# Sigmoid attention and a swish layer on one core: a hand-ordered kernel written anew as a table of tasks

## The chip, the cores and the metric

The kernel runs on one core of a Trainium2 chip. The metric is the device time of one execution in microseconds (us). A core has TensorE (PE, the matmuls), ScalarE (ACT, here the sigmoids), VectorE (DVE), GpSimd (POOL, which here issues the loads) and SyncE (SP, which here issues the stores). TensorE writes to PSUM, which has eight banks; ScalarE and VectorE read it.

## The reference

Eight sequences of 448 tokens, 12 heads of 64 columns; then two dense layers over all 3584 tokens, 768 to 2048 to 768. There is no softmax: each weight of the attention is a sigmoid by itself.

```python
scores = scale * np.matmul(q, k.transpose(0, 1, 3, 2)) - np.log(S)
attn = 1.0 / (1.0 + np.exp(-scores))
x = np.matmul(attn, v)                         # to (B * S, H * D)
h = x @ w_in
g = h * (1.0 / (1.0 + np.exp(-beta * h)))
out = g @ w_out
```

## The kernel before

All inputs are cast to 16 bits by the loads. The eight sequences are called batches (b); the 12 heads of a batch make three groups of four heads (`g`, 24 in all), and a group has two slots of two heads. The work comes in these units:

- **Loads and transposes.** `load_one` and `load_v` (L111, L132, L139) bring q, k and v; `load_w_in` and `load_w_out` (L149, L157) the weights. VectorE transposes q and k of a group in blocks of 32 (L177, L193).
- **Scores.** The 448 keys are three blocks of 128 and a last one of 64 (`jt` = 0 to 3). `visit` computes one block of a group in 8 matmuls of 448 columns (L208; four of them lie side by side in the array); the last block of two groups goes together, in 16. ScalarE then takes the sigmoid of two heads at once, 128 x 896 (L219). For batch 0, `half_visit` does the same with the queries in two halves of 224 columns.
- **Attention output.** `attend` sums over the keys in 16 matmuls (L278), and VectorE casts the result to `xT` (L287).
- **First layer.** `dense1(b, dc)`: 128 of the 2048 hidden columns of one batch, 6 matmuls of 448 columns (L296), a sigmoid on ScalarE (L304), a product on VectorE (L307) into `gt`. For batch 0 it is done in halves of 224 columns.
- **Second layer.** 28 tiles of 128 tokens. Tiles 0, 1, 2 and 27 are plain (`dense2`, L326): 16 matmuls of 384 columns for each half of the output, tile 27 split into 512 and 256. The other 24 go by pairs through `strassen` (L408): seven products of 8 matmuls of 384 columns in place of eight, with sums of hidden blocks (L397) and of weight blocks (L372) and sums of results (L427 and following) on VectorE.

The order is written by hand. The main loop goes over the visits; between them it takes units of the two layers from one stream (`filler_stream`), by a budget of microseconds for each visit. In the start-up, as long as no weights are there, matmuls on zeros (`idle_units`, L521, 28 in all) stand between the half visits. PSUM is split by use: three double banks for scores and two single ones in the start-up, then two double ones and four single ones (`share_psum`); `bank` hands out the single ones in turn, and `held` keeps those that a pair of tiles adds up in.

```python
for g in range(QPB):
    for second in range(2):
        half_visit(g, 0, second)
        if 2 * g + second < 2 * QPB - 1:
            idle_units(4 if g < QPB - 1 else 2)
```

Of the kernel before, what the change touches and what calls it, by code (L numbers as in the profile page):

```python
# [9 lines left out]
FP16 = mybir.dt.float16  # L10


@with_exitstack
def kernel(
# [10 lines left out]
    nc = tc.nc  # L25
    AF = mybir.ActivationFunctionType
    ALU = mybir.AluOpType

    B, H, S, D = q.shape
    NTOK, DM = out.shape  # L30
    DFF = moe_w_in.shape[1]
    P = 128
    BLK = 32
    HQ = P // BLK
    NB = S // BLK
    PAIR = D // BLK
    JF = S // P
    KL = S - JF * P
    NF = JF * P // BLK
    NPAIR = H // 2  # L40
    QPB = H // HQ
    NHC = DM // P
    NDC = DFF // P
    HALF = DM // 2
    WIN = 2 * S
    NTILE = WIN // P
    QH = S // 2
    MSCALE = 1.0 / math.sqrt(D)
    NEG_LOG_S = -math.log(float(S))
    NSLOT = B * NPAIR  # L50
    NQUAD = B * QPB

    const = ctx.enter_context(tc.tile_pool(name="const", bufs=1))
    rawp = ctx.enter_context(tc.tile_pool(name="rawp", bufs=3))
    vp = ctx.enter_context(tc.tile_pool(name="vp", bufs=2))
    qTp = ctx.enter_context(tc.tile_pool(name="qTp", bufs=4))
    kTp = ctx.enter_context(tc.tile_pool(name="kTp", bufs=4))
    attnp = ctx.enter_context(tc.tile_pool(name="attnp", bufs=12))
    xTp = ctx.enter_context(tc.tile_pool(name="xTp", bufs=3))
    sump = ctx.enter_context(tc.tile_pool(name="sump", bufs=3))  # L60
    sigp = ctx.enter_context(tc.tile_pool(name="sigp", bufs=3))
    outp = ctx.enter_context(tc.tile_pool(name="outp", bufs=4))
    psum = {}
    used = {}
    held = {}

    def share_psum(pools: ExitStack, n_sc: int, n_one: int):
        for name, bufs in (("sc", n_sc), ("one", 1)):
            psum[name] = pools.enter_context(
                tc.tile_pool(  # L70
                    name=f"ps_{name}{n_sc}",
                    bufs=bufs,
                    space=bass.MemoryType.PSUM,
                    reuse_waits="tile",
                )
            )
        used.clear()
        used.update((i, i - n_one) for i in range(n_one))

    def touch(i: int):  # L80
        used[i] = max(used.values()) + 1


    def bank(name: str, cols: int = S, hold=None):
        i = min((i for i in used if i not in held.values()), key=used.get)
        touch(i)
        if hold is not None:
            held[hold] = i
        return psum["one"].tile([P, cols], FP32, tag=f"one{i}", name=name)


    nlogs = const.tile([P, 1], FP32, name="nlogs")
    dummy = const.tile([P, 1], FP32, name="dummy")
    beta_in = const.tile([BLK, P], FP32, name="beta_in")
    beta_sb = const.tile([P, BLK], FP32, name="beta_sb")
    w_in16 = const.tile([P, NHC, DFF], FP16, name="w_in16")
    w_out16 = const.tile([P, NDC, DM], FP16, name="w_out16")

    raws = {}
    vs = {}

    def load_one(g: int, r: int, c0: int = 0, c1: int = NB, h0: int = 0, h1: int = HQ):
        b, t = divmod(g, QPB)
        if g not in raws:
            raws[g] = rawp.tile([P, 2, NB, D], FP16, tag="raw", name="raw")  # L110
        nc.gpsimd.dma_start(  # L111
            out=raws[g][h0 * BLK : h1 * BLK, r, c0:c1].rearrange("p c d -> p (c d)"),
            in_=(q, k)[r][b, HQ * t + h0 : HQ * t + h1].rearrange(
                "h (p c) d -> (h p) (c d)", c=NB
            )[:, c0 * D : c1 * D],
        )

    def load_qk(g: int):
        load_one(g, 0)
        load_one(g, 1)  # L120

    def swapped(g: int) -> int:
        return int(g > QPB and g % 2 == 1)

    def last_base(s: int) -> int:
        return (s % 2 ^ swapped(s // 2)) * KL

    def load_v(b: int):
        vs[b] = vp.tile([P, H, JF + 1, D], FP16, tag="v16", name="v16")
        rows = v[b].rearrange("h (p c) d -> p h (c d)", c=NB)  # L130
        for i in range(HQ):
            nc.gpsimd.dma_start(  # L132
                out=vs[b][i * BLK : (i + 1) * BLK, :, 0:JF].rearrange("p h j d -> p h (j d)"),
                in_=rows[:, :, JF * i * D : JF * (i + 1) * D],
            )
        rows = v[b].rearrange("h (p c) d -> p h c d", c=NB)
        for c in range(NF, NB):
            lo = (c - NF) * BLK
            nc.gpsimd.dma_start(out=vs[b][lo : lo + BLK, :, JF], in_=rows[:, :, c])  # L139

    def double_v_last(b: int):
        nc.vector.tensor_copy(out=vs[b][KL:P, :, JF], in_=vs[b][0:KL, :, JF])

    WCH = 8
    WOUT = 2

    def load_w_in(c: int):
        n = DFF // WCH
        nc.gpsimd.dma_start(  # L149
            out=w_in16[:, :, c * n : (c + 1) * n],  # L150
            in_=moe_w_in[:, c * n : (c + 1) * n].rearrange("(c p) f -> p c f", p=P),
        )

    def load_w_out(c: int, half: int):
        n = NDC // WOUT
        cols = slice(half * HALF, (half + 1) * HALF)
        nc.gpsimd.dma_start(  # L157
            out=w_out16[:, c * n : (c + 1) * n, cols],
            in_=moe_w_out[c * n * P : (c + 1) * n * P, cols].rearrange("(c p) f -> p c f", p=P),
        )  # L160

    qT = {}
    kT = {}
    at_tiles = {}
    xTs = {}

    def in_order(b: int, t):  # L170
        t = t.rearrange("p c e -> p (c e)").bitcast(FP32)
        return t.rearrange("p (q c) -> p c q", c=NB) if b == B - 1 else t

    def transpose_q(g: int, c0: int = 0, c1: int = NB, rows=slice(0, P)):
        if g not in qT:
            qT[g] = qTp.tile([P, NB * BLK, PAIR], FP16, tag="qT", name="qT")
        nc.vector.transpose(  # L177
            out=in_order(g // QPB, qT[g][rows, c0 * BLK : c1 * BLK]),
            in_=raws[g][rows, 0, c0:c1].rearrange("p c d -> p (c d)").bitcast(FP32),
        )  # L180

    def transpose_k(g: int, last: int, rows=slice(0, P)):
        if g not in kT:
            kT[g] = kTp.tile([P, S, PAIR], FP16, tag="kT", name="kT")
        to = kT[g][rows].rearrange("p k e -> p (k e)").bitcast(FP32)
        frm = raws[g][rows, 1].rearrange("p c d -> p (c d)").bitcast(FP32)
        frm = frm.rearrange("p (c f) -> p c f", c=NB)
        if last:
            to, frm = to[:, JF * P :], frm[:, NF:].rearrange("p c f -> p (c f)")
        else:  # L190
            to = to[:, 0 : JF * P].rearrange("p (j i q) -> p i j q", j=JF, i=HQ)
            frm = frm[:, 0:NF].rearrange("p (i j) f -> p i j f", j=JF)
        nc.vector.transpose(out=to, in_=frm)  # L193

    def transpose(g: int, r: int):
        if r == 0:
            transpose_q(g)
        else:
            transpose_k(g, 0)
            transpose_k(g, 1)  # L200

    def score_tile():
        return psum["sc"].tile([P, 2, 512], FP32, tag="sco", name="sco")

    def score(sco, u0: int, s: int, jt: int, hh: int, e: int, c0: int, n: int):
        g, lo = s // 2, (s % 2 * 2 + hh) * BLK
        base, nk = (last_base(s), KL) if jt == JF else (0, P)
        nc.tensor.matmul(  # L208
            sco[base : base + nk, hh, u0 : u0 + n],
            kT[g][lo : lo + BLK, jt * P : jt * P + nk, e],  # L210
            qT[g][lo : lo + BLK, c0 : c0 + n, e],
            start=(e == 0),
            stop=(e == PAIR - 1),
            tile_position=(lo, base),
        )

    def weigh(sco, n: int):
        at = attnp.tile([P, 2, S], FP16, tag="attnT", name="attnT")
        nc.scalar.activation(  # L219
            out=at[:, :, 0:n],  # L220
            in_=sco[:, :, 0:n],
            func=AF.Sigmoid,
            bias=nlogs[:, 0:1],
            scale=MSCALE,
        )
        return at


    def visit(g: int, jt: int, also=()):
        if jt < JF:  # L230
            todo = [(score_tile(), [s]) for s in (2 * g, 2 * g + 1)]
        else:
            todo = [(score_tile(), [2 * h, 2 * h + 1]) for h in (g, *also)]
        for e in range(PAIR):
            for sco, slots in todo:
# [82 lines left out]
    def dense2(t: int, half: int, part: int):  # L318
# [14 lines left out]
        if part < N2 - 1:  # L333
            return
# [343 lines left out]
```

## Time and profile before

| | |
|---|---|
| time, median of 3 runs | 391.84 us (390.23 to 391.84) |
| the profiled execution: time, span | 392.5 us, 390.7 us |
| mean granted TensorE clock | 0.996 |
| busy: TensorE, ScalarE, VectorE, GpSimd | 98%, 62%, 59%, 17% |
| chain that ended last: TensorE, ScalarE, VectorE, DMA | 94%, 2%, 1%, 1% |
| matmuls; sigmoids of scores; second-layer products | 2988; 171; 672 and 128 plain |
| loaded into the core, HBM read | 22.81 MB, 45.62 MB |

The span is the time from the first to the last instruction of the profiled execution; the time holds 1.8 us more. The groups of the profile are by source line, engine and shape, with the busy time of all and the mean of one; an instruction of ScalarE or VectorE overlaps the next one by some 0.1 us, so a mean is longer than the distance from start to start. In the timeline a line holds several instructions of one kind in a row.

### The profile page before, as it was taken

How to read it: one execution, taken by the hardware profiler on the slowest of the kernel's cores; microseconds unless marked ns; L12 is line 12 of the kernel's file. 1: busy time of each engine (PE TensorE's matmuls, PEld its weight loads, DVE VectorE, ACT ScalarE, POOL GpSimd, SP SyncE). 2: the span in 40 equal slices, each digit the busy share in tenths (PEclk: the TensorE clock that was granted, in tenths of full speed). 3: DMA queues.
4: the chain of work that ended last, by engine and by line, in shares of the span. 5: the costliest groups of instructions: out<-in, count | busy, mean ns of one | idle time of the engine just before them, and what ended most of it. 6: DMA issues, size and time to landing. Idle time of an engine off the chain costs nothing.

```text
span 390.7 us, 7374 instructions
## 1 busy us (share of the span) xinstructions
PE 382.7 (98%) x2988; PEld 191.5 (49%) x2988; DVE 231.0 (59%) x440; ACT 241.8 (62%) x329; POOL 68.4 (17%) x119
## 2 busy tenths in 40 slices
PE   7999999999999999999999999999999999999996
PEld 2367754444544444544544445544445444555563
DVE  3255555775676555755765656665676655655762
ACT  3879757588654786587564793658853677625200
POOL 7833333104100410131110410104100000000000
PEclk9899999999999999999999999999999999999999
DMA  7999999539133672438243472539113300030033
GB/s 95 181 190 204 197 204 198 104 87 119 26 87 64 130 78 40 88 72 89 47 93 72 92 75 46 115 75 140 19 30 82 81 3 2 0 82 0 2 81 121
DMA packets 42433, 34.30 MB, mean 88 GB/s; under 512 B 21904, under 2 KB 38816, under 8 KB 42400
## 3 DMA queue, kind: packets, MB, share of 16 engines
q0 software_dynamic: 37008, 22.81, 42.6%
q1 hardware_dynamic: 5392, 11.02, 11.0%
q8 instruction: 23, 0.38, 0.4%
q14 instruction: 10, 0.08, 0.1%
HBM read 45.62 MB, written 11.01 MB: 145 GB/s over the span
## 4 chain that ended last, share of the span: by engine, by line
PE 94%; ACT 2%; DVE 1%; DMA 1%; POOL 0%; issue 0%; POOLq 0%
PE m_ps L296 38%; PE m_ps L408 29%; PE sco L208 12%; PE av_ps L278 10%; PE m_ps L326 4%; ACT attnT L219 2%; PE idle_ps L521 1%; DMA raw<-in_k_dram 1%; POOL raw L111 0%; DVE gt L307 0%; DVE qT L177 0%; DVE kT L193 0%; ACT sg L304 0%; DVE xT L287 0%; DVE osb L339 0%
## 5 line engine op out<-in xcount | busy, mean ns | idle before, releaser
L219 ACT ACTIVATE attnT<-sco,nlogs 128x896 f16<-128x896 f32 (+1 forms) x171 | 160.5, 991 | 85.4 <-PE sco L208 84.8
L296 PE MATMUL m_ps<-xT,w_in 128*128 128x448 f16 (+1 forms) x864 | 154.7, 332 | 0.4 <-DVE gt L307 0.3
L307 DVE TENSOR_TENSOR gt<-m_ps,sg 128x448 f16<-128x448 f32 (+1 forms) x144 | 79.8, 572 | 85.3 <-ACT sg L304 85.2
L296 PEld LDWEIGHTS <-w_in 128*128 128x128 f16 x864 | 80.6, 98 | 70.9 <-issue 15.5
L304 ACT ACTIVATE sg<-m_ps,beta_sb 128x448 f32<-128x448 f32 (+1 forms) x144 | 82.1, 595 | 31.3 <-PE m_ps L296 30.1
L408 PEld LDWEIGHTS <-sum 128*128 128x128 f16 x480 | 45.2, 98 | 36.4 <-issue 7.9
L208 PE MATMUL sco<-qT,kT 32*128 32x448 f16 (+3 forms) x864 | 53.6, 342 | 3.2 <-DVE kT L193 1.8
L408 PE MATMUL m_ps<-w_T,sum 128*128 128x384 f16 x288 | 51.6, 327 | 0.0
L111 POOL DMA_DIRECT2D raw<-in_q_dram x28 | 15.5, 554 | 195.2 <-DVE kT L193 189.2
L427 DVE TENSOR_TENSOR osb<-m_ps,osb 128x384 f32<-128x384 f32 x60 | 33.3, 555 | 18.7 <-PE m_ps L408 16.9
L287 DVE CAST xT<-av_ps 128x448 f16<-128x448 f32 (+1 forms) x54 | 28.8, 568 | 23.9 <-PE av_ps L278 23.9
L278 PE MATMUL av_ps<-attnT,v 128*64 128x448 f16 (+3 forms) x432 | 42.2, 340 | 0.1
L397 DVE TENSOR_TENSOR sum<-gt 128x1024 f16<-128x1024 f16 x60 | 39.2, 679 | 0.1
L408 PE MATMUL m_ps<-w_T,gt 128*128 128x384 f16 x192 | 34.2, 326 | 0.0
L408 PE MATMUL m_ps<-w_out,sum 128*128 128x384 f16 x192 | 33.7, 326 | 0.0
L278 PEld LDWEIGHTS <-v 128*64 128x64 f16 (+1 forms) x432 | 19.1, 107 | 24.7 <-issue 15.5
L208 PEld LDWEIGHTS <-kT 32*128 32x128 f16 (+1 forms) x864 | 13.9, 96 | 33.0 <-issue 28.5
L408 PEld LDWEIGHTS <-gt 128*128 128x128 f16 x192 | 18.1, 98 | 14.7 <-issue 3.1
L326 PE MATMUL m_ps<-w_out,gt 128*128 128x384 f16 (+2 forms) x128 | 22.5, 327 | 0.0
L132 POOL DMA_DIRECT2D v<-in_v_dram x32 | 19.8, 636 | 7.4 <-DMA w_in<-in_moe_w_in_dram 5.7
L193 DVE STREAM_TRANSPOSE kT<-raw 128x384 f32<-128x384 f32 (+3 forms) x50 | 17.6, 387 | 3.7 <-DMA raw<-in_k_dram 3.6
L177 DVE STREAM_TRANSPOSE qT<-raw 128x448 f32<-128x448 f32 (+2 forms) x28 | 17.0, 608 | 2.6 <-DMA raw<-in_q_dram 2.6
(23 smaller groups left out, 91.0 us busy)
## 6 DMA issues: line engine op xcount, KB each, us to landing
out_dram<-osb SPq DMA_DIRECT2D x98, 96.0 KB, 1.9
raw<-in_k_dram POOLq DMA_DIRECT2D x23, 224.0 KB, 5.1
raw<-in_q_dram POOLq DMA_DIRECT2D x21, 224.0 KB, 3.6
v<-in_v_dram POOLq DMA_DIRECT2D x32, 144.0 KB, 6.2
w_in<-in_moe_w_in_dram POOLq DMA_DIRECT2D x8, 384.0 KB, 10.5
w_out<-in_moe_w_out_dram POOLq DMA_DIRECT2D x4, 768.0 KB, 14.2
v<-in_v_dram POOLq DMA_DIRECT2D x16, 48.0 KB, 5.9
out_dram<-osb SPq DMA_DIRECT2D x2, 384.0 KB, 2.3
```

The costliest lines, as they stand in the source:

```text
L132: nc.gpsimd.dma_start(out=vs[b][i * BLK : (i + 1) * BLK, :, 0:JF].rearrange("p h j d -> p h (j d)"), in_=rows[:, :, JF * i * D : JF * (i + ...
L208: nc.tensor.matmul(sco[base : base + nk, hh, u0 : u0 + n], kT[g][lo : lo + BLK, jt * P : jt * P + nk, e], qT[g][lo : lo + BLK, c0 : c0 + n ...
L219: nc.scalar.activation(out=at[:, :, 0:n], in_=sco[:, :, 0:n], func=AF.Sigmoid, bias=nlogs[:, 0:1], scale=MSCALE,)
L278: nc.tensor.matmul(av[hh * D : (hh + 1) * D, 0:n], vs[b][base : base + nk, 2 * (s % NPAIR) + hh, jt], at[base : base + nk, hh, 0:n], start ...
L287: nc.vector.tensor_copy(out=xTs[b][:, s % NPAIR, c0 : c0 + n], in_=av[:, 0:n])
L296: nc.tensor.matmul(m1[:, 0:n], w_in16[:, hc, dc * P : (dc + 1) * P], xTs[b][:, hc, c0 : c0 + n], start=(hc == 0), stop=(hc == NHC - 1),)
L304: nc.scalar.activation(out=sg[:, 0:n], in_=m1[:, 0:n], func=AF.Sigmoid, bias=0.0, scale=beta_sb[:, dc : dc + 1])
L307: nc.vector.tensor_tensor(out=gt[:, dc, off : off + n], in0=m1[:, 0:n], in1=sg[:, 0:n], op=ALU.mult)
L326: nc.tensor.matmul(m2, gt[:, dc, cols(t)], w_out16[:, dc, lo:hi], start=(dc == 0), stop=(dc == NDC - 1),)
L397: nc.vector.tensor_tensor(out=sums[t, i], in0=x, in1=y, op=op)
L408: nc.tensor.matmul(m2, (x if op is None else sums[t, i])[:, dc], w[:, dc], start=first and dc == 0, stop=(dc == ND - 1), skip_group_check= ...
L427: nc.vector.tensor_tensor(out=out, in0=in0, in1=in1, op=op)
```

## The change

The kernel is written anew. A class `Work` lists the work as tasks, each with its engine, the tasks that it waits for, the buffers and banks that it takes and gives back, and a cost in microseconds. The order of TensorE and the order of the loads stand in the file as two strings of names, `PE_ORDER` (461 tasks) and `LOAD_ORDER` (113). When the program is built, `plan` runs through these lists with the costs: it fixes the order of ScalarE, VectorE and SyncE (what is ready first goes first) and hands out the buffers and banks. `Emitter` then writes the instructions in that order. Names: `i0` the idle matmuls, `h1.0.1` a half visit (group, half of the queries, which one), `s6.0` a visit (group, block of keys), `a6.0.0` an attention output (group), `d1.6.0` a unit of the first layer (batch, dc, half), `t0.2.1` half a product of the second layer (pair of tiles, product, part); `q`, `k`, `v`, `wi`, `wo` are loads.

What differs in the work:

- All 28 tiles go by pairs through the seven products; there are no plain tiles. `T3` and `T4` overwrite `B12` and `B21` of the weights.
- One set of 14 idle matmuls at the start in place of 28 in eight places.
- PSUM is one pool of eight banks. A score visit takes two pairs of neighbouring banks (`"DD"`), a unit of the first layer one, an attention output two, a pair of tiles one for each of the four results as it opens.
- The order of all units is another; the batches of the first layer and the pairs of tiles of the second interleave, and pairs overlap at the end. The start-up begins with group 1, the loads with a quarter of v. The output weights come after the queries and keys of group 5.
- Buffers: 10 tiles of attention weights in place of 12, two of `xT` in place of three.
- The branch that would do the first layer in seven products too (`quads`) is in the file but not taken, since `WINO` is empty.

```diff
+WINO = ()
...
+SLOTS = {"raw": 3, "v": 2, "xT": 2, "qT": 4, "kT": 4, "attn": 10, "sg": 3, "sum": 3, "osb": 4, "S7": 3, "xs": 1}
+ENGINES = ("PE", "ACT", "DVE", "POOL", "SP", "Z")
...
+    def half_visit(self, g, c0, second):
+        k, part = self.k, c0 // QH
+        slots = (2 * g, 2 * g + 1)
+        if second:
+            plan = [(s, 2, i, 0) for i, s in enumerate(slots)] + [(s, JF, 0, QH) for s in slots]
+            us, widths = 2 * (mm(QH) + WAVE) + SWITCH + 2 * (mm(QH) + WAVE), (S, QH)
+            deps = self.k_first[g] + self.k_last[g]
+            groups = [(plan, "DD", 2, us, f"h{g}.{part}.1")]
+        else:
+            plan = [(s, jt, i, jt * QH) for jt in (0, 1) for i, s in enumerate(slots)]
+            us, widths = 4 * (mm(QH) + WAVE), (S, S)
+            deps = self.k_first[g]
+            groups = [(plan, "DD", 2, us, f"h{g}.{part}.0")]
...
+        self.beta = self.add("DVE", "beta", (0.5, 0.75), [], lambda t: k.turn_beta())
+        for i, n in enumerate((14,)):
+            t = self.pe_task(f"i{i}", n * 0.216, mode="d", banks="S")
+            t.emit = lambda t, n=n: k.idle(t.bank[0], n)
+            t.give_banks = [(t, 0)]
+        for g in range(QPB):
+            self.group_loads(g, True)
+        self.v_loads(0)
+        self.w_loads()
...
+def plan(work, pe_names, load_names):
+
+    by = work.by
+    queue = {"PE": [by[n] for n in pe_names], "POOL": [by[n] for n in load_names]}
+    at = {"PE": 0, "POOL": 0}
...
+            if kind == "D":
+                for x in range(7):
+                    if not (bank_busy[x] or bank_busy[x + 1] or x in got or x + 1 in got):
+                        key = (x % 2, max(bank_free[x], bank_free[x + 1]))
+                        if best is None or key < best[0]:
+                            best = (key, x)
+                if best is None:
+                    return None
+                got += [best[1], best[1] + 1]
+                mend += [False, False]
...
+            if e in queue:
+                if at[e] >= len(queue[e]):
+                    continue
...
+                cand = [t for t in ready[e] if can(t)]
+                if not cand:
+                    continue
+                t = min(cand, key=lambda t: (ready_at[t.i] - t.soon, t.i))
+                ready[e].remove(t)
+                begin(t, now)
...
+PE_ORDER = """
+i0 h1.0.1 h1.0.0 h2.0.1 h2.0.0 h0.0.00 h0.0.1 h0.0.01 a1.0.0 a1.0.1 h2.1.0 a0.0.0 a0.0.1 h0.1.0 a2.0.0 a2.0.1 h0.1.1
+h2.1.1 d0.9.0 d0.4.0 h1.1.1 d0.8.0 a0.1.0 h1.1.0 a2.1.0 a0.1.1 s3.1 a1.1.0 a1.1.1 s3.0 a2.1.1 d0.10.0 d0.11.0 d0.5.1
+s3.2 d0.7.1 d0.2.0 d0.6.0 d0.7.0 s3.3 d0.0.1 d0.5.0 s4.1 a3.0.0 s4.2 d0.1.1 d0.2.1 d0.9.1 d0.15.0 s4.0 d0.11.1 d0.14.0
+d0.1.0 d0.14.1 s4.3 d0.6.1 d0.12.0 s5.0 a4.0.0 s5.1 d0.10.1 d0.3.0 d0.13.1 s5.2 d0.12.1 d0.8.1 d0.13.0 d0.3.1 a5.0.0
+d0.4.1 d0.0.0 d0.15.1 d1.6.0 d1.7.0 d1.0.0 d1.1.0 d1.10.0 d1.2.0 d1.8.0 d1.15.0 d1.12.0 d1.4.0 d1.11.0 d1.5.0 d1.14.0
+t0.0.0 t0.0.1 t0.1.0 t0.1.1 t0.2.0 t0.2.1 s6.0 t0.3.0 t0.3.1 d1.9.0 s6.1 t0.4.0 d1.3.0 d1.13.0 t0.4.1 s6.2 t0.5.0
...
+d3.11.0 d3.13.0 s14.2 d3.7.0 d3.2.0 s14.1 a13.0.0 t5.0.0 t5.0.1 t5.1.0 s14.0 t5.1.1 t5.2.0 t5.2.1 t5.3.0 t5.3.1 s14.3
+t5.4.0 t5.4.1 a14.0.0 s15.0 t5.5.0 t5.5.1 t5.6.0 t5.6.1 d4.2.0 d4.10.0 s15.2 d4.7.0 d4.4.0 s15.1 d4.8.0 d4.13.0 d4.6.0
...
+t12.5.0 t12.5.1 t13.2.0 t13.2.1 t12.6.0 t13.3.0 t12.6.1 t13.3.1 t13.4.0 t13.4.1 t13.5.0 t13.5.1 t13.6.0 t13.6.1
...
+LOAD_ORDER = """
+v0.0 q1.0.0 k1.0.0 q2.0.0 k2.0.0 v0.1 q0.0.0 v0.5 k0.0.0 q0.0.2 k0.0.2 v0.4 v0.2 v0.3 q2.7.0 q1.7.0 q0.7.0 v1.0 wi4
+wi2 q3.0.0 wi1 k3.0.0 v1.3 wi5 wi3 q4.0.0 v1.1 k4.0.0 wi0 v1.2 v1.4 v1.5 wi7 q5.0.0 wi6 k5.0.0 wo11 wo10 wo01 wo00
+v2.0 q6.0.0 v2.3 v4.0 v2.4 q10.0.0 q9.0.0 v4.5 k6.0.0 v2.2 q7.0.0 k9.0.0 v2.1 v2.5 k10.0.0 v4.2 k7.0.0 q8.0.0 k8.0.0
...
+        self.ws["T3"], self.ws["T4"] = B12, B21
...
+        self.still = self.sum[-1].rearrange("p a b -> p (a b)")
+        self.ps = psum.tile([P, 8, 512], FP32, name="ps")
+
+    def bank(self, i, n=S):
+        return self.ps[:, i, 0:n]
...
+    def begin(self):
+        nc = self.nc
+        nc.vector.memset(self.still[:, 0:512], 0.0)
+        nc.vector.memset(self.dummy, 0.0)
+        nc.vector.memset(self.nlogs, NEG_LOG_S)
+        nc.vector.memset(self.beta_in, 0.0)
+        nc.scalar.activation(out=self.dummy, in_=self.dummy, func=AF.Sigmoid, bias=0.0, scale=1.0)
+        nc.sync.dma_start(out=self.beta_in[0:NDC], in_=self.beta.rearrange("(c p) -> c p", p=P))
+
+    def idle(self, x, n):
+        for _ in range(n):
+            self.nc.tensor.matmul(self.bank(x, 512), self.still[:, 0:P], self.still[:, 0:512], start=True, stop=True)
...
+    def scores(self, units, side, c0, n):
+        for i in range(0, len(units), side):
+            for e in range(PAIR):
+                for s, jt, d, u0, q, k in units[i : i + side]:
+                    base, nk = (self.last_base(s), KL) if jt == JF else (0, P)
+                    for hh in range(2):
+                        lo = (s % 2 * 2 + hh) * BLK
+                        self.nc.tensor.matmul(
+                            self.ps[base : base + nk, d + hh, u0 : u0 + n],
+                            self.kT[k][lo : lo + BLK, jt * P : jt * P + nk, e],
+                            self.qT[q][lo : lo + BLK, c0 : c0 + n, e],
+                            start=(e == 0),
+                            stop=(e == PAIR - 1),
+                            tile_position=(lo, base),
+                        )
...
+    def product(self, t, i, part, x, slot):
+        a, _, _, w = self.operands(t, i)
+        if slot is not None:
+            a = self.sum[slot]
+        for dc in range(part * ND // 2, (part + 1) * ND // 2):
+            self.nc.tensor.matmul(
+                self.bank(x, HALF),
+                a[:, dc],
+                w[:, dc],
+                start=(i < 4 and dc == 0),
+                stop=(dc == ND - 1),
+                skip_group_check=i >= 4,
+            )
...
+    def weigh(self, d, slot, n):
+        self.nc.scalar.activation(
+            out=self.at[slot][:, :, 0:n],
+            in_=self.ps[:, d : d + 2, 0:n],
+            func=AF.Sigmoid,
+            bias=self.nlogs[:, 0:1],
+            scale=MSCALE,
+        )
...
+    psum = ctx.enter_context(tc.tile_pool(name="psum", bufs=1, space=bass.MemoryType.PSUM))
+    emitter = Emitter(tc.nc, const, psum, q, k, v, moe_w_in, moe_w_out, moe_beta, out)
+    work = Work(emitter)
+    work.build()
+    order, _, missing = plan(work, PE_ORDER.split(), LOAD_ORDER.split())
+    assert not missing, missing
...
+        emitter.begin()
+        for t in order:
+            if t.emit:
+                t.emit(t)
```

## The prediction

> **What bounds the kernel now.** First the page: which engine is full, and where.
>
> ```profile
> PE 382.7 (98%) x2988; PEld 191.5 (49%) x2988; DVE 231.0 (59%) x440; ACT 241.8 (62%) x329; POOL 68.4 (17%) x119
> ACT  3879757588654786587564793658853677625200
> PEclk9899999999999999999999999999999999999999
> ```
>
> TensorE is the only full engine; ScalarE is at 62%, densest in the first 60 us. A busy TensorE is not one at its peak, so the second view is the chain that ended last, for the pace where nothing waits:
>
> ```profile
> 346.04 18.16 PE m_ps L296 x96
> 364.20 18.20 PE m_ps L408 x112
> 382.40 5.21 PE m_ps L326 x32
> ```
>
> 96 first-layer matmuls of 448 columns took 18.16 us, 0.189 each; 112 of 384 columns took 18.20, 0.1625 each. The chain joins on to the last matmul at 387.61; the span ends at 390.7, so 3.1 us follow it. Third, the timeline of TensorE, for the price of a change of kind and for waits:
>
> ```profile
> 60.14 0.37 PE L208 MATMUL sco<-qT,kT 32*128 32x448 f16 x2
> 60.80 0.57 PE L208 MATMUL sco<-qT,kT 32*128 32x448 f16 x6 [0.28 <-ACT attnT L219]
> ...
> 79.18 1.12 PE L296 MATMUL m_ps<-xT,w_in 128*128 128x448 f16 x5
> ...
> 108.57 1.64 PE L278 MATMUL av_ps<-attnT,v 128*64 128x448 f16 x16
> 110.14 0.57 PE L208 MATMUL sco<-qT,kT 32*128 32x448 f16 x8
> 110.65 2.12 PE L408 MATMUL m_ps<-w_T,sum 128*128 128x384 f16 x12
> 112.71 0.57 PE L208 MATMUL sco<-qT,kT 32*128 32x448 f16 x8
> ```
>
> Start to start: a whole attention output (16 matmuls) 1.57 us, a score visit 0.51, and 12 matmuls of 384 take 2.06, which is 12 x 0.1625 + 0.11: each change of kind costs 0.11. The scores at 60.80 wait for ScalarE to empty a bank. Such stalls come until 72.64; behind 79.18 every piece of the timeline starts where its price says, up to the end. So the kernel is two stretches: until 79.18 a start-up in which TensorE also waits and fills with idle matmuls, then 308.4 us (79.18 to 387.61) of gapless TensorE.
>
> Fourth, ScalarE and the loads of the start-up:
>
> ```profile
> 10.42 1.53 ACT L219 ACTIVATE attnT<-sco,nlogs 128x896 f16<-128x896 f32 x2 [1.20 <-PE sco L208]
> 12.75 8.76 ACT L219 ACTIVATE attnT<-sco,nlogs 128x896 f16<-128x896 f32 x10 [0.80 <-PE sco L208]
> ...
> 43.42 1.90 ACT L219 ACTIVATE attnT<-sco,nlogs 128x896 f16<-128x896 f32 x2 [0.43 <-PE sco L208]
> 45.22 1.46 ACT L304 ACTIVATE sg<-m_ps,beta_sb 128x224 f32<-128x224 f32 x4
> ```
>
> Two 896-column sigmoids take 1.90 at 1.00 each, so they start 0.90 apart; a 448-column one adds 0.52 (1.53 with its own tail of 0.63); four of 224 columns take 1.46, so 0.34 apart. Twice in the first 22 us the list of ScalarE is short of scores, then it is full for ten tiles.
>
> **The change, part by part.**
>
> *Seven products for tiles 0, 1, 2 and 27.* Four plain tiles are 128 matmuls; two more pairs are 112: 16 x 0.1625 = 2.6 us of TensorE saved, all on its path. The price lies on others: 10 sums (0.68) and 12 adds (0.555) on VectorE less 8 copies (0.56), and two ScalarE copies (0.48). VectorE goes from 231 to about 240 of 390 us: hidden, and at worst late by one 0.68 sum at a pair's start.
>
> *The listed order behind the start-up.* I cut the new list after d0.15.1, the last first-layer unit of batch 0. Before it stand all attention of batches 0 and 1 and all of d0; behind it everything else. At the prices above the list behind the cut adds up to 321 us: 112 units d of 1.131 (126.7), 196 half products of 0.65 (127.4), the rest of the visits and outputs, and 0.11 for each change of kind. The cross-check is the old trace: at 79.18 the same work was done, plus one visit (0.6 with its switch) and tiles 0 to 2 (6 x 2.6 = 15.6); 308.4 + 0.6 + 15.6 - 2.6 = 322. I take 321. This part is *longer* than the old gapless stretch by 12.6 us; the change wins only if the cut comes over 12.6 us before 79.18.
>
> *Does it stay gapless?* Between the last scores and their attention output the list leaves 1.5 us at the least (s14.3 to a14), mostly 2.5 to 6; the first tile is read 0.6 behind the visit's start (visit 42.81, sigmoid 43.42) and takes 1.0, so it is there 1.1 behind its end. Between a batch's last unit d and the pair that reads it 2.2 us or more, against 0.63 for the sigmoid and 0.62 for the gate (groups by shape). In stretches of 12 us of list ScalarE has at most 10.9 to do and VectorE 7.5. But the banks are tight: two score tiles take four of eight, a pair of tiles holds two to four, an output wants two. The old trace has no stall there to price it by: 0 (as it is now) to 0.28 (the bank wait above) for each of some 40 visits, 11 us. I take 0.7, near the old value, since half or more of the visits come with two banks held.
>
> *The start-up.* Now 14 idle matmuls in one go, none between visits (28 before), so TensorE has only real work. Its list from the first attention output a1.0.0 to d0.15.1 is 11 us to s3.1, 26.5 from there to a5.0.0 and 3.3 to the cut. ScalarE's work up to a5.0.0: batch 0 has 18 tiles of 896 (0.90) and 6 of 448 (0.52), 19.3; batch 1 has 21 of 896, 18.9; 25 sigmoids of 224 at 0.34, 8.4: 46.6 us. So ScalarE, not TensorE, sets this stage. When does it begin? The list of loads puts 144 KB of v and then q and k of group 1 (112 + 224) first: 480 KB before the first score. Here the old trace shows what had landed when:
>
> ```profile
> 4.90 0.57 DVE L193 STREAM_TRANSPOSE kT<-raw 64x384 f32<-64x384 f32 x1 [1.00 <-DMA raw<-in_k_dram]
> ...
> 8.41 0.41 DVE L177 STREAM_TRANSPOSE qT<-raw 128x224 f32<-128x224 f32 x1 [0.32 <-DMA raw<-in_q_dram]
> 9.71 0.70 DVE L193 STREAM_TRANSPOSE kT<-raw 128x384 f32<-128x384 f32 x2 [0.89 <-DMA raw<-in_k_dram]
> ```
>
> 168 KB at 4.9, 448 at 8.4, 672 at 9.7: 480 KB at 8.6; with transposes (0.7), scores (0.65) and hand-over (0.2) the first sigmoid starts at 10.2, four later than now (6.14). If the three larger transfers run from 3 us on at the 150 to 180 GB/s that the page has for 10 us and later, it is 7.8. I take 9.4. From there to k of group 5 the loads amount to 7.3 MB, at the page's 195 GB/s there by 42 us, about 3 to 5 us ahead of its scores: off the path. Two edits of the load queue have one answer: v4.0 now stands ahead of k of group 6 and must wait for the slot that a5.0.0 frees (58), and POOL holds all later loads with it; the 0.95 MB up to that k land some 7 us later, and its scores come at about 80. The two memsets that go from POOL to VectorE (0.16 each) lie ahead of all data.
>
> ScalarE without a gap: 9.4 + 46.6 + 0.2 = 56.2 for a5.0.0. TensorE is nearly as full (a1.0.0 can't start before the ninth tile is read, about 16.7; 16.7 + 11 + 26.5 = 54.2), so both will lose to each other: the ten tiles from 12.75 took 8.76 where 8.2 to 8.3 is the work, 0.95; the mixed stretch from 23 to 39 us has 13.2 us of work in 15.7, 0.84. The list is nearer to the first kind (one sort of wait, eight banks): 0.96 gives 9.4 + 46.6 / 0.96 + 0.2 = 58.1, and the cut at 61.4.
>
> *The end.* The last product now ends in a 384-column subtraction (0.555, before 0.42) and a store of 384 KB (lands in 2.3, before 128 KB in 1.7): 3.1 + 0.7 = 3.8.
>
> **Sum.** 61.4 + 321 + 0.7 + 3.8 = 386.9 of span, against 390.7. The profiled execution took 392.5 in all, 1.8 more than its span, and lies 0.7 above the median of 391.84: 386.9 + 1.8 - 0.7 = 388.0. Without a gap on ScalarE and with the early start (7.8 + 46.6 + 0.2 + 3.3 + 321 + 3.8 = 382.7) it is 383.8.
>
> **Rivals.** *ScalarE starves in the start-up (slower).* If its queue, in the order of the table, is as full as in the mixed stretch, 0.84, a5.0.0 comes at 9.4 + 55.5 + 0.2 = 65.1, and the time is 395.0. At 0.89 nothing is gained any more, below 0.86 it is slower by over 0.5%. For it: a late start, and TensorE nearly as full. Against it: no idle matmuls, no plain tiles in between.
>
> *The clock.* In the window from 9 to 12 us the granted clock was 0.50:
>
> ```profile
> 9.00:12.00 3.00, 3.00 (x21) 0.75 (x20) 1.63 (x5) 1.75 (x3) 1.86 (x4) 0.50 1.22 171
> ```
>
> It followed a stretch with 1.5 us without a matmul; the fillers after it are gone now. If TensorE gets half the clock for one such window (3.4 us) in the 11 us before s3.1, that is 1.7 us; for all of them 11 us, time 399. The Trainium skill (TensorE: Matmul & The Clock Gate, part 1) has the clock halved after an idle window of about 3.4 us and released after a busy one; the trace agrees on the length (8.7 to 12.1) but not on the idleness, as that window had matmuls in it. By that rule one window, not all, would be lost.
>
> *Bank waits in the long stretch.* 0.28 at each of 40 visits: 11 us, 398. Against it: the same eight banks, and 308 us without one.
>
> *The list isn't what is run.* The branch for the first layer is switched off (WINO is empty), so no saving comes from there; the seven products are in the list 14 times.
>
> **How the numbers follow.** Forecast, queue at over 0.92: 0.56, its own range 383.8 to 389.9. ScalarE between 0.86 and 0.92, within 0.5% (about 2 us, what a measurement here can tell from no change): 0.19. ScalarE at 0.86 or less: 0.12. Bank waits: 0.08. Clock over several windows: 0.05. So faster 0.56, same 0.19, slower 0.25. The range runs from the gapless case to the first slow rival, which leaves the dearest cases out.
>
> **What would show it.** First sigmoid at 9 to 10 us; a5.0.0 near 58; the first layer of batch 1 in one block from about 61; no gaps on TensorE from there; 3.8 us behind the last matmul. A cut later than 65, or TensorE waits of over 4 us behind it, make it wrong.

## The result, and the profile after

The changed kernel takes 401.88 us (median of 4 runs, 401.18 to 403.56) against 391.84: a ratio of 1.027 (95% interval 1.022 to 1.032). It is slower, where a gain of 1% was forecast. Its profiled execution took 401.18 us, with a span of 399.4.

The page of the changed kernel, its busy times, then the rows of 40 slices for TensorE and its clock:

```profile
PE 381.7 (96%) x2958; PEld 191.9 (48%) x2958; DVE 236.3 (59%) x456; ACT 241.7 (61%) x331; POOL 69.1 (17%) x117
## 2 busy tenths in 40 slices
PE   6899999999996999997999999988999999999996
...
PEclk9589999999999999998999999999999999999999
```

TensorE is busy for about as long as before (382.7) in a span that is 8.7 us longer. The loss isn't in the start-up but in slices 13, 19, 27 and 28 (counted from 1). Three stages, by the timeline and the chain of both kernels:

| stage | before | predicted | after |
|---|---|---|---|
| first sigmoid of scores | 6.14 | 9.4 | 9.93 |
| a5.0.0 (the output that ends ScalarE's start-up work) starts | 77.1 | 58.1 | 58.75 |
| the cut (batch 0's first layer and all attention of batch 1 done) | 79.18 | 61.4 | 62.06 |
| from the cut to the last matmul's end | 308.4 | 321.7 | 333.4 |
| behind the last matmul | 3.1 | 3.8 | 3.9 |
| span | 390.7 | 386.9 | 399.4 |

The start-up came out within 0.7 us, the end within 0.1. The long stretch is 11.7 us over its forecast. The timeline of TensorE has four waits of over 0.4 us in it (the bracket gives the idle time ahead, and what ended it):

```profile
128.63 3.74 PE L883 MATMUL ps<-xT,w_in 128*128 128x448 f16 x12 [3.07 <-DVE gt L901]
182.53 2.40 PE L883 MATMUL ps<-xT,w_in 128*128 128x448 f16 x6 [2.33 <-DVE gt L901]
268.32 4.70 PE L883 MATMUL ps<-xT,w_in 128*128 128x448 f16 x24 [1.49 <-DVE gt L901]
275.94 2.43 PE L883 MATMUL ps<-xT,w_in 128*128 128x448 f16 x12 [1.17 <-DVE gt L901]
```

Together 8.1 us, each for a VectorE product that empties a bank. The chain of waits of the changed kernel shows the first of them from its root:

```profile
117.85 0.63 POOL v L789
...
119.66 7.15 DMA raw<-in_k_dram
126.81 0.02 issue
126.83 0.58 DVE kT L832
127.41 0.51 DVE gt L901
...
128.63 3.74 PE ps L883 x12
```

TensorE waits for a product, the product for a transpose of k that stands ahead of it on VectorE, the transpose for a load that took 7.15 us from its issue, and that load for a v load ahead of it on GpSimd. Ahead of the other three waits VectorE stood in the same way: 1.67 us for q (at 180.29), 2.54 for k (267.06) and 2.81 for the copy of the last rows of a v (273.82). Why the v load at the root of the first was so late, the timeline of GpSimd says:

```profile
117.22 1.25 POOL L789 DMA_DIRECT2D v<-in_v_dram  x2 [29.46 <-PE ps L867]
...
170.14 0.61 POOL L789 DMA_DIRECT2D v<-in_v_dram  x1 [45.74 <-PE ps L867]
...
258.95 1.83 POOL L789 DMA_DIRECT2D v<-in_v_dram  x3 [10.16 <-PE ps L867]
```

Three times GpSimd stood for 10 to 46 us on a v load whose buffer an attention output (L867) had yet to free, with all later loads behind it; then about ten loads went out at once. Each wait of TensorE ends 9 to 17 us behind such a release.

The rest of the loss is the clock. In the rows by stretch of the changed kernel the granted clock (the figure behind the busy times) falls to 0.50 at 127.9, near the end of the first wait:

```profile
126.00:127.00 1.00, 0.00 (x0) 0.00 (x0) 0.17 (x1) 0.84 (x2) 0.00 (x0) 1.00 1.13 280
...
129.00:130.00 1.00, 1.00 (x4) 0.40 (x3) 0.10 (x1) 0.00 (x0) 0.00 (x0) 0.50 1.15 199
```

It stays there for 3.4 us, and again from 182.5, the end of the second wait. The 12 matmuls from 128.63 took 3.7 us where 2.3 is their price: 1.4 us lost; 1.6 at the second: 3.0. So 333.4 = 321 + 8.1 + 3.0 + 1.3; the 1.3 is a rest without a row of its own.

### The profile page after: what moved, and what is told of

It reads as the page before. It is cut to its first block, busy times and chain, and to the rows that moved or that the text cites. A ratio compares the mean times of both kernels' runs of the same rounds, so it can differ in the third digit from the quotient of the medians.

```text
span 399.4 us, 7347 instructions
## 1 busy us (share of the span) xinstructions
PE 381.7 (96%) x2958; PEld 191.9 (48%) x2958; DVE 236.3 (59%) x456; ACT 241.7 (61%) x331; POOL 69.1 (17%) x117
## 3 DMA queue, kind: packets, MB, share of 16 engines
q0 software_dynamic: 37008, 22.81, 41.6%
## 4 chain that ended last, share of the span: by engine, by line
PE 84%; DMA 8%; ACT 3%; DVE 2%; issue 2%; POOL 1%; DVEq 0%; POOLq 0%
PE ps L883 33%; PE ps L1003 32%; PE ps L867 10%; PE ps L845 10%; DMA v<-in_v_dram 3%; DMA raw<-in_k_dram 3%; ACT attn L855 2%; DMA raw<-in_q_dram 2%; POOL v L789 1%; DVE gt L901 1%; DVE kT L832 0%; ACT sg L892 0%; POOL v L793 0%; DVE qT L818 0%; DVE osb L901 0%
## 5 line engine op out<-in xcount | busy, mean ns | idle before, releaser
L855 ACT ACTIVATE attn<-ps,nlogs 128x896 f16<-128x896 f32 (+1 forms) x171 | 160.0, 1002 | 61.6 <-PE ps L845 59.5
L883 PE MATMUL ps<-xT,w_in 128*128 128x448 f16 (+1 forms) x864 | 157.1, 335 | 8.6 <-DVE gt L901 8.1
L892 ACT ACTIVATE sg<-ps,beta_sb 128x448 f32<-128x448 f32 (+1 forms) x144 | 82.2, 606 | 63.6 <-PE ps L883 49.8
L901 DVE TENSOR_TENSOR gt<-ps,sg 128x448 f16<-128x448 f32 (+1 forms) x144 | 78.3, 566 | 66.4 <-ACT sg L892 66.1
L1003 PE MATMUL ps<-w_T,sum 128*128 128x384 f16 x336 | 60.9, 327 | 0.0
L845 PE MATMUL ps<-qT,kT 32*128 32x448 f16 (+3 forms) x864 | 55.7, 358 | 3.7 <-DVE kT L832 2.5
L867 PE MATMUL ps<-attn,v 128*64 128x448 f16 (+3 forms) x432 | 43.9, 349 | 0.3 <-ACT attn L855 0.3
L901 DVE TENSOR_TENSOR osb<-ps,osb 128x384 f32<-128x384 f32 x70 | 38.5, 551 | 7.6 <-PE ps L1003 6.7
L1003 PE MATMUL ps<-w_out,gt 128*128 128x384 f16 x224 | 41.1, 327 | 0.0
L1003 PE MATMUL ps<-w_out,sum 128*128 128x384 f16 x224 | 40.2, 326 | 0.0
L867 PEld LDWEIGHTS <-v 128*64 128x64 f16 (+1 forms) x432 | 19.8, 110 | 26.9 <-issue 19.6
L832 DVE STREAM_TRANSPOSE kT<-raw 128x384 f32<-128x384 f32 (+3 forms) x50 | 18.7, 388 | 11.7 <-DMA raw<-in_k_dram 11.6
L818 DVE STREAM_TRANSPOSE qT<-raw 128x448 f32<-128x448 f32 (+2 forms) x28 | 17.1, 610 | 7.5 <-DMA raw<-in_q_dram 7.5
```

What stands on the lines that cost most here:

```text
L818: self.nc.vector.transpose(out=self.in_order(g, self.qT[slot][rows, c0 * BLK : c1 * BLK]), in_=self.raw[raw][rows, 0, c0:c1].rearrange("p ...
L832: self.nc.vector.transpose(out=to, in_=frm)
L845: self.nc.tensor.matmul(self.ps[base : base + nk, d + hh, u0 : u0 + n], self.kT[k][lo : lo + BLK, jt * P : jt * P + nk, e], self.qT[q][lo ...
L855: self.nc.scalar.activation(out=self.at[slot][:, :, 0:n], in_=self.ps[:, d : d + 2, 0:n], func=AF.Sigmoid, bias=self.nlogs[:, 0:1], scale= ...
L867: self.nc.tensor.matmul(self.bank(x, n)[hh * D : (hh + 1) * D], self.vs[v][base : base + nk, 2 * (s % NPAIR) + hh, jt], self.at[at][base : ...
L883: self.nc.tensor.matmul(self.bank(x, n), self.w_in16[:, hc, dc * P : (dc + 1) * P], self.xT[xT][:, hc, c0 : c0 + n], start=(hc == 0), stop ...
```

## The experiments

Theory A is the chain above: held loads. Rival B: the banks are too tight and the order wrong whatever the loads do. Rival C: the loads might stay held, but VectorE's order, worked out with loads that land too early, is at fault. The ratios are to the kernel before.

**Another list of loads.** Edit: behind `wo00`, q and k by group, the v of a batch behind q and k of its third group.

```diff
-v2.0 q6.0.0 v2.3 v4.0 v2.4 q10.0.0 q9.0.0 v4.5 k6.0.0 ...
+q6.0.0 k6.0.0 q7.0.0 k7.0.0 q8.0.0 k8.0.0 v2.0 v2.1 ... v2.5 q9.0.0 k9.0.0 ...
```

> Only the list of loads is changed, behind the last of the output weights: q and k by group, the v of a batch behind the q and k of its third group. Theory A (the load queue: a v load waits on GpSimd for the slot that an attention output frees, all later loads wait behind it, and transposes that wait for them stand on VectorE ahead of the products that empty PSUM banks): the four waits of TensorE on VectorE (8.1 us) and the two half-clock windows behind them (3.1 us) go; the order of VectorE that is worked out anew puts transposes ahead of the weight sums near 77 us, which costs some 3 us; time 392 to 395. Theory B (banks too tight and VectorE's order wrong whatever the loads do): the waits stay near 125, 180 and 270 us; 400 or more.

408.19 us, 1.043 (1.039 to 1.048). A's number is missed; B's (400 or more) came true, and TensorE still waits for products near the places that B names: 3.58 us at 136, 1.59 at 190, 2.13 at 277. By itself this run speaks for B. The timeline of VectorE shows the same kind of wait by another load:

```profile
134.19 0.35 DVE L797 COPY v<-v 64x768 f16<-64x768 f16 x1 [6.63 <-DMA v<-in_v_dram]
134.58 2.22 DVE L901 TENSOR_TENSOR gt<-ps,sg 128x448 f16<-128x448 f32 x4
```

With two buffers the v of batch 3 still waits for an attention output (issued at 124.4); the copy of its last rows waits for it on VectorE, with four products behind it, and TensorE stood for the 3.58 us. The weight sums cost 2.7 more near 80 us, as expected. So the list alone doesn't mend it. The trace lets A stand in a wider form, that any load which is issued late and has its VectorE user placed early does this; the next runs test that.

**A third buffer for v, orders worked out anew.** Edit, in `SLOTS`:

```diff
-"v": 2
+"v": 3
```

> The list of loads as in the changed kernel, but three buffers for v in place of two, so that a v load waits less for an attention output. Theory A: the long holds of GpSimd (29, 46, 10 us) shrink, the waits of TensorE behind 100 us and the half-clock windows go with them; 390 to 393. Theory B: the waits stay; 400 to 402.

392.29 us, 1.000 (0.998 to 1.003): 9.6 less, and no wait of TensorE behind the start-up. The banks are the same, so B falls; but VectorE's order was worked out anew as well.

**Later landings in the plan.** Edit:

```diff
-dma_free = max(dma_free, now + 1.83) + ...
+dma_free = max(dma_free, now + (1.83 if now < 60 else 6.5)) + ...
```

> The list of loads and the buffers as in the changed kernel; the costs by which VectorE's order is worked out let loads behind 60 us land 4.7 us later, so that transposes stand further back on VectorE. Theory A (the held loads are the cause): the products come ahead, but the scores now wait for the late loads themselves; TensorE loses 4 us or more behind 100 us, time 396 to 402. Theory C (the loads could stay held, only VectorE's order is wrong): the waits go; 390 to 393.

395.08 us, 1.008 (1.005 to 1.010): between the two. In the profile, the slowest execution of the five (396.92), GpSimd is held as before (41.6 us at the longest), but TensorE's waits on products shrink to 0.2 us; 2.6 us of waits for transposes behind 90 us and 3.4 us of half clock at the first of them take their place, and a5.0.0 comes only at 61.06. So C holds in part: with the loads held, the place of the transposes on VectorE decides whether one wait becomes a stop of everything behind it.

**The same orders, a third buffer.** To part A from C: plan with two buffers, then hand the v loads three in turn. Every engine has the changed kernel's order, task by task.

```diff
+    for i, b in enumerate((0, 1, 2, 4, 3, 5, 6, 7)):
+        work.v_first[b].slot["v"] = i % 3
```

> Every order is the changed kernel's, instruction for instruction on each engine, planned with two buffers for v; only the v loads go to three buffers in turn, so that they needn't wait for the attention outputs. Theory A (the held loads): all four waits of TensorE and the half-clock windows behind them go, 389 to 393. Theory C (VectorE's planned order is wrong in itself): waits stay, 396 or more.

391.74 us, 0.996 (0.994 to 0.999): 10.1 us less than the changed kernel by nothing but an earlier issue of the loads. VectorE's timeline here, for the transpose that had waited at 126.83, still between the same products:

```profile
122.08 0.62 DVE L902 TENSOR_TENSOR gt<-ps,sg 128x448 f16<-128x448 f32 x1 [2.47 <-ACT sg L893]
122.62 0.57 DVE L833 STREAM_TRANSPOSE kT<-raw 128x384 f32<-128x384 f32 x1
123.11 0.58 DVE L902 TENSOR_TENSOR gt<-ps,sg 128x448 f16<-128x448 f32 x1
```

No wait on it. The order was harmless as soon as the load was early: with this order, the held loads are the cause. The profiled execution is the fastest of ten (388.86 us, granted clock 0.985, half clock from 10.4 to 20.6 us). Its span is 387.1, where the prediction had 386.9. But seven of the ten had clocks of 0.971 to 0.976 and took 391.3 to 392.2; the runs on fillers below ask why.

**Two buffers, both repairs of the order.** Edit: the list of the first experiment, landings behind 60 us 3.2 us later in the plan, transposes of the groups behind the first layer ranked lower (`late` is -20 for them):

```diff
-self.add("DVE", f"tk{g}.0", turn_us(384), [ld["k", g, 0, 0]], take=["kT"])
+self.add("DVE", f"tk{g}.0", turn_us(384), [ld["k", g, 0, 0]], take=["kT"], soon=late)
...
-dma_free = max(dma_free, now + 1.83) + ...
+dma_free = max(dma_free, now + (1.83 if now < 60 else 5.0)) + ...
```

> Two buffers for v; the loads in the order of need as in the run of the load order alone (408 us), but VectorE's order is worked out with loads behind 60 us landing 3.2 us later and with the transposes ranked 20 us lower. If that run's waits came from VectorE instructions standing ahead of the products while they wait for a load (a v copy 6.6 us), they go: no TensorE wait of over 1.5 us behind 90 us, 390 to 394. If the order of TensorE itself is at fault, 400 or more.

392.16 us, 1.000 (0.997 to 1.003). One wait of TensorE of 0.4 us behind 60 us is left. The third buffer isn't needed if the list and the places on VectorE fit together.

**More idle matmuls at the start.** Edit:

```diff
-for i, n in enumerate((14,)):
+for i, n in enumerate((26,)):
```

> 26 idle matmuls at the start in place of 14, up to the first scores. If ScalarE sets the start-up, as the prediction had it, the clock of TensorE there matters little: 401 to 402.5, a5.0.0 within 0.5 us of 58.75. If the half clock from 8.4 to 22 us sets it, a5.0.0 comes 1.5 us or more earlier and the time is 400 or less.

404.99 us, 1.034 (1.029 to 1.039); a5.0.0 at 60.09 in place of 58.75. Both expectations missed: the half clock didn't shrink, it moved (from 8.4 to 22 us, to 14.7 to 28.4).

**Fillers between the half visits**, with the third buffer. Edit, in the idle matmuls and in `PE_ORDER`:

```diff
-(14,)
+(24, 3, 3, 3, 3, 3,)
...
-i0 h1.0.1 h1.0.0 h2.0.1 h2.0.0 h0.0.00 h0.0.1 h0.0.01
+i0 h1.0.1 h1.0.0 i1 h2.0.1 i2 h2.0.0 i3 h0.0.00 i4 h0.0.1 i5 h0.0.01
```

> Three buffers for v, with 24 idle matmuls at the start and three behind each of the next five half visits. If the half clock of the start-up (about 20 us of it with three buffers and no fillers, 392.3 us) costs time, less of it is left and a5.0.0 comes at 58.5 or earlier in place of 60.2: 389 to 391. If ScalarE alone sets the start-up, the fillers only take its banks: 392 to 394.

389.82 us, 0.994 (0.991 to 0.996), 2 us below the runs with three buffers and no fillers; a5.0.0 at 58.77, 0.3 later than hoped. The rows by stretch of the changed kernel, then of this one:

```profile
10.00:20.00 10.00, 8.86 (x108) 4.13 (x104) 4.78 (x14) 9.15 (x12) 8.96 (x14) 0.50 1.29 154
```

```profile
10.00:20.00 10.00, 9.06 (x117) 4.04 (x116) 5.20 (x14) 9.15 (x12) 8.48 (x14) 1.00 1.31 162
```

TensorE's busy share is nearly the same, the clock twice. ScalarE (the fourth busy time, 9.15) is as busy in both: in these 10 us it sets the pace. What the clock costs shows in the time from the first sigmoid to a5.0.0: 48.4 and 48.8 us in the two profiles whose half clock ended by 22 us, 50.8 to 51.6 in the six where it ended between 26.7 and 30.5, 49.3 here with none (49.5 to 50.3 in the three later runs with fillers). So half clock up to 22 us was hidden, and 1 to 3 us go with what lies behind it. The executions of one kernel say the same: with three buffers and no fillers, those at a granted clock of 0.985 and 0.986 took 388.9 us, those at 0.971 to 0.974 391.4 to 393.1.

**The first v later**, with the third buffer. Edit, in the list of loads:

```diff
-v0.0 q1.0.0 k1.0.0 q2.0.0 k2.0.0 v0.1 ...
+q1.0.0 k1.0.0 q2.0.0 k2.0.0 v0.0 v0.1 ...
```

> Three buffers for v, and the first quarter of v is loaded behind q and k of group 2 in place of ahead of everything. The first sigmoid comes about 1 us earlier (144 KB less ahead of it). If the start-up is ScalarE's from its first sigmoid on, a5.0.0 comes up to 1 us earlier, 391 to 392; if q and k of group 0 are waited for instead, nothing moves, 392 to 393.

390.09 us, 0.994 (0.991 to 0.997), 0.9 below the expected range. The first sigmoid comes at 7.57 in place of 9.28, a5.0.0 at 58.42 in place of 60.23.

**Both together**, once with three buffers and the changed kernel's order, once with two and the repaired one (18 idle matmuls at the start, since the first scores come earlier):

> Three buffers for v as in the run with the same orders, 18 idle matmuls at the start, three behind each of the next five half visits, and the first quarter of v loaded behind q and k of group 2. If the two gains of the start-up (clock, earlier first sigmoid; each some 2 us) add up: 387 to 389, clock above 0.995. If they buy the same thing, because both only bring q, k and TensorE in step with ScalarE: 389 to 390.5.

> Two buffers for v, the loads in the order of need with VectorE's order worked out for later landings, plus the fillers and the later first quarter of v. If the third buffer is only one way to keep loads ahead of their users, this comes within 1 us of the run with three buffers and the same start-up: 387 to 390.

388.61 us, 0.993 (0.990 to 0.995), and 388.89 us, 0.993 (0.991 to 0.995). Both are faster than both kernels, the one before by 0.7%. The gains of the start-up add up in part (3.1 us below the run with the same orders; counted from there, the gains by themselves make 3.6), and a third buffer or a repaired order come to the same.

**The fillers in the changed kernel alone.**

> The changed kernel with the fillers of the start-up alone (24 at the start, three behind each of the next five half visits); loads and buffers are its own. If the held loads are worth 10 us and the clock of the start-up 2 to 2.5, apart from each other: 398.5 to 400.5, with the TensorE waits near 125, 180 and 270 us still there. If the waits shift with the start-up, 395 or less, or over 402.

402.99 us, 1.029 (1.025 to 1.033): no gain, and a miss, since the waits didn't shift. The four are at the places named (129, 183, 269, 277 us), 8.5 us of them; a5.0.0 comes at 59.35. That fits the run before: the changed kernel's half clock ended at 22 us in its profile, where it cost nothing, and its other executions had much the same granted clock (0.969 to 0.973), so the fillers had nothing to win. It is argued from these clocks and not shown, as only one execution of the changed kernel was profiled.

## Why the prediction was wrong

- **The pace and the start-up** came out as taken, the pace in part by luck. ScalarE's 46.6 us of work took 48.6 (first sigmoid 9.93, a5.0.0 58.75, hand-over 0.2): a queue 0.96 full, as taken. In the six profiles whose half clock ended later the same work took 50.8 to 51.6, about 0.91. The later start (0.5 us) is nearly the whole miss of the cut (0.7). The gain of 17.1 us over the old start-up is there in the trace.
- **The list behind the cut** was right: 333.4 less the waits and the clock is 322.3, against 321. The seven products saved what they should: 2958 matmuls, 14 of the 30 fewer being idle ones and 16 those of the four tiles.
- **"Does it stay gapless?"** is the step that failed: it put 0.7 us for waits, where 8.1 were lost, and 3.0 more by the clock that fell at them. The rival "bank waits" had about the sum (11 us) but not the way: not 40 small waits for tight banks but four long ones, gone with the same banks once the loads were early.
- **Its root is the sentence on the load queue**, "two edits of the load queue have one answer". It follows one held v load (v4.0) to its last victim and finds cover, which was right: nothing waited there. The list holds GpSimd again at v3.0, v5.0 and v7, and there the q, k or v behind it is due within 9 to 17 us of the release. v4 ahead of v3 with two buffers means that v3 can't be loaded before batch 2 is through: readable in the two lists, and not read. The cover that was reckoned, of ScalarE and VectorE by their work, says nothing of an instruction that waits at the head of VectorE with the products behind it.
- **The landing time** was the second half. The plan lets a load land after 1.83 us and its bytes at the full rate. In the burst behind 117 us the k of 224 KB, behind 0.48 MB, was 7.15 us from issue, with later loads and stores under way beside it; what each of them took of that isn't shown.
- **The clock** was put on the wrong stage. Its half rate in the start-up lasted 13.7 us, and was hidden under ScalarE in this profile; the 3.0 us came at the waits. With the loads early it is a price after all: the run with the same orders is 0.4% below the kernel before by its median, where 1% was forecast, and fillers win 2 us more.

Against 390.7 the sum is now: start-up 17.1 us shorter, the list behind the cut 12.6 longer as reckoned and 1.3 on top (its rest), waits 8.1, clock 3.0, end 0.8 longer: 8.7 us more.

## What to carry to other kernels

A list of loads on one in-order queue has to be followed to every load that waits for a buffer, and for each the question is who stands behind it and how soon that is due; one such check that comes out well says nothing of the next. A user of a load on an in-order engine belongs behind whatever empties PSUM, or the load well ahead of it. Here the early loads alone brought back 10.1 us, the later users alone 6.8; a new list that left both undone cost 6.3 more. And a wait of 2 to 3 us of TensorE should be priced with half the clock for 3.4 us behind it, which followed most of them here.

## What the runs showed of the hardware

Half clock followed stops of TensorE that were shorter than the 3.4 us that it lasts at a time: the first was 2.3 us old when the clock fell, at 127.9, and most of the half rate ran over matmuls. In all traces behind 60 us, it came with each of the six stops of 2.3 to 3.6 us, with three of the six between 1.8 and 2.2, and with none of the five between 1.2 and 1.6. Why stops of about 2 us went both ways stays open. The Trainium skill (TensorE: Matmul & The Clock Gate, part 1) has the clock fall after an idle window of about 3.4 us; the length agrees, but in the 3.4 us ahead of 127.9 TensorE was busy for 1.1, so the idle share was two thirds only.

In the start-up TensorE was busy for 8.9 of 10 us by its records and yet kept half the clock, with score matmuls of 32 rows and half-width outputs in it; with 24 full-width idle matmuls ahead of them and 15 among them it was at 1.00, at 9.1 of 10 us busy. 26 ahead and none among them only moved the half clock to 14.7 us. So the busy share in the records doesn't tell the granted clock; which part of the score work it leaves out isn't shown.
